# A new order for all engines from a corrected tally, and later v in four transfers, in a windowed attention with a gated feed-forward layer

## The chip, the cores and the metric

The kernel runs on one core of a Trainium2 chip. The metric is the device time of one execution in microseconds. It was 347.35 us in the median of three runs (346.08 to 350.0).

## The reference

Inputs are q, k and v of 8 batches, 8 heads, 576 positions and 64 dimensions in float32, a value weight and an output weight of 512 x 512, and a depthwise convolution of 5 taps on 512 channels.

```
scores = (q @ k.T) / 8, and only 0 <= i - j < 64 is kept
attn   = softmax(scores)                # the sum has 1e-9 added
x      = attn @ v                       # heads side by side: 8 x 576 x 512
gate   = sigmoid(sum over 5 taps of conv_w[tap] * x shifted)   # causal, per channel
out    = (gate * (x @ w_val)) @ w_out
```

The three weights come as float64 words and are taken apart in the kernel.

## The kernel before

**Attention.** The window is 64, so a block of 64 queries meets two blocks of keys. A score group (S, line 529) covers two query blocks of all 8 heads with 32 small float32 products of 64 x 32 by 96 columns. VectorE (DVE) adds the mask and takes the maximum (M, line 547), ScalarE (ACT) makes the exponent and the sums (X, line 559), GpSimd (POOL) and DVE make the reciprocal (Ra, Rb), one of DVE, POOL or ACT multiplies by it (N, lines 579 and 581), and DVE transposes (T, line 593). There are 36 score groups. A batch is cut into two halves of 256 and 320 positions (or 320 and 256), and for each half TensorE (PE) makes the product with v in many small matmuls (AV, line 630).

**Convolution.** Its taps run on DVE (C, line 718), but for three quarters of the first batch on PE, as products with diagonal matrices (K, line 693; the diagonals DG are built at line 897).

**Feed-forward.** x and h are each split into a high and a low part in float32r, and so are the two weights, so every product is three: V (line 772) and O (line 842) are runs of 12 matmuls. x is split by XH and XL, h by HH and HL (line 804).

**Weights.** A 512 x 512 weight comes as four column or row blocks. Each block passes through nine steps, named by a letter: `h` (head, lines 443 and 445), `k` (clamp, line 448), `b`, `c`, `H`, `p`, `l`, `r` (line 475) and `s` (line 478). w0 to w3 are the value weight, w4 to w7 the output weight, cw the convolution's.

**The order of the work.** It is written out by a planner in the program (`in_order`) before the kernel is built: each operation has a cost on each engine that may run it (`flex`, or one engine by `on`), a priority with a hand-searched adjustment for each operation (`adj`), its dependencies and its buffers. The planner goes through them with a clock of its own and gives each engine one list, which the chip then runs in order. Transfers are one more list, on the queue of SyncE (SP). The clock of the planner also holds `Fetch`: PE's instructions come in blocks of a given size (`block`), and a block that is run too soon after the last one is late. Where PE would be idle in the first 120 us, the planner puts in dummy products of the identity (`warm`, line 250), two rows in the profile for each. Loads are named LQ (q and k of one half), LV (v of a batch; of the first batch in two parts, LV0_0 and LV0_1) and LW (weights: the value weight in four quarters LW0_0 to LW1_1, the output weight in two halves LW2 and LW3), LC (the convolution's weights) and DO (output rows). A lower priority number goes first among those that are ready.

Of the kernel before, what the change touches and what calls it, by code (L numbers as in the profile page):

```python
# [29 lines left out]
    flex=dict(EO='AV', HH='AV', HI='AV', C='AV', EX='AV', XH='AVG', XL='GV', CC='AV', DG='GV', HL='GV', N='GVA', WR='GV', WH='AV', TL='AVG', WK='GV', HA='AV'),  # L30
# [17 lines left out]
    drain=165,  # L48
    held=30,
# [55 lines left out]
def in_order(ops, room):  # L105
# [8 lines left out]
    ready = {}  # L114
    for op in ops:
        if not op.left:
            for e in op.cost:
                ready.setdefault(e, []).append(op)
    out, done = [], set()
    bus = port_at = 0.0  # L120
    mode = "F"
    fetch = Fetch()
    since, until, margin, each = CFG["awake"]
    total = len(ops)

    shared = {}

    def earliest(op, e):
        t = max(free_at.get(e, 0.0), ready_time(op, e))
        if op.share is not None and e in op.on:  # L130

            t = max(t, shared.get((op.share, "V" if e == "A" else "A"), 0.0) + 60.0)
        if e in op.port:
            t = max(t, port_at)
        return t

    while len(out) < total:
        best = None
        for e, c in ready.items():
            c[:] = [op for op in c if op not in done]  # L140
            pick, cand = None, []
            for op in c:
                t = earliest(op, e)
                if len(op.cost) > 1 and e != min(
                        op.cost, key=lambda x: earliest(op, x) + op.cost[x] + CFG["bias"].get(x, 0)):
                    continue
                for kind, c_ in op.needs:
                    s = slots[kind]
                    t = max(t, s[c_ - 1]) if len(s) >= c_ else float("inf")
                if t == float("inf"):  # L150
                    continue
                late = 0.0
                if e == "P":
                    late = fetch.run(t, op.n, op.cost[e] / op.n, bus, False) - t - op.cost[e]
                k = (t + late - (CFG["wait"] if e == "P" and op.prio < CFG["ffn_prio"] else 0)
                     - (CFG["stay"] if e == "P" and "F" != mode and op.mode != "F" else 0), op.rank)
                cand.append((k, op))
# [10 lines left out]
        if e == "P" and op.mode != mode:  # L168
            t += CFG["drain"]
# [40 lines left out]
def tile_window_attention_gated_ffn(  # L210
# [134 lines left out]
    def at_of(g):  # L345
        return g * 12.0 / NB
# [653 lines left out]
```

## Time and profile before

| | |
|---|---|
| median of three runs | 347.35 us (346.08 to 350.0) |
| profiled execution | 345.73 us, span 343.9 us |
| mean granted TensorE clock | 0.979 |
| PE busy | 317.9 us (92%) |
| DVE busy | 269.4 us (78%) |
| ACT busy | 238.5 us (69%) |
| POOL busy | 175.7 us (51%) |

Busy is the time in which at least one instruction of that engine ran. Matmuls overlap, so the sum of their durations is more than the busy time. PEld is PE's weight loads, beside the matmuls. "issue" as the cause of a wait means that the engine waited for nothing that the profile shows. A releaser is inferred from semaphores. A granted clock of 1.00 is the upper of TensorE's two levels, 0.50 the lower.

### The profile page before, as it was taken

The page shows a single profiled execution, that of the slowest core. Times are in us where ns is not written, and L with a number is a line of the kernel's source. Part 1 is how long each engine was busy: PE and PEld are TensorE (multiplying, and loading weights), DVE is VectorE, ACT ScalarE, POOL GpSimd, SP SyncE. Part 2 cuts the span into 40 slices and gives each one's busy share as a digit, 9 for nine tenths or more (in the row PEclk, how much of TensorE's full clock was granted, in tenths as well). Part 3 has the DMA queues.
Part 4 walks back from the last instruction along what each step waited for, and adds up shares of the span by engine and source line. Part 5 has one row for each costly group of instructions (what it writes and reads, how often), then busy time and mean ns, then how long its engine had stood idle before and what let it go on. Part 6 is the DMA issues. An engine that isn't in the chain of part 4 may idle for free.

```text
span 343.9 us, 15255 instructions
## 1 busy us (share of the span) xinstructions
PE 317.9 (92%) x6280; PEld 277.2 (81%) x6280; DVE 269.4 (78%) x1088; ACT 238.5 (69%) x867; POOL 175.7 (51%) x225
## 2 busy tenths in 40 slices
PE   6687795989989999999999999989999999989995
PEld 5576584968978988898888888978898879978984
DVE  3887895779979796899798985979899878867300
ACT  1775795788588994487769796868639678734421
POOL 6355654554823663556523751857635264744510
PEclk9699997899999999999999999999999999999999
DMA  7969662273357031852564144750291100011012
GB/s 230 280 194 366 153 204 89 73 222 83 89 135 231 11 125 63 217 186 89 191 149 133 44 176 135 236 189 34 60 278 37 64 33 35 2 63 63 2 61 91
DMA packets 30117, 43.99 MB, mean 128 GB/s; under 512 B 2528, under 2 KB 23264, under 8 KB 30048
## 3 DMA queue, kind: packets, MB, share of 16 engines
q1 hardware_dynamic: 30048, 43.02, 41.1%
q8 instruction: 49, 0.80, 1.0%
q14 instruction: 20, 0.16, 0.1%
HBM read 33.57 MB, written 9.44 MB: 125 GB/s over the span
## 4 chain that ended last, share of the span: by engine, by line
PE 87%; DVE 4%; issue 3%; DMA 2%; POOL 1%; SPq 1%; ACT 0%; ACTq 0%
PE v L772 31%; PE o L842 30%; PE s L529 10%; PE av L630 10%; PE g L693 5%; DMA qk_b<-in_kT_dram 2%; DVE pb L547 2%; PE s L250 1%; POOL w3m L448 1%; PE g L692 0%; DVE pts L593 0%; PE g L250 0%; DVE wv_lo L478 0%; DVE xl L732 0%; SPq L373 0%
## 5 line engine op out<-in xcount | busy, mean ns | idle before, releaser
L559 ACT ACTIVATE pb<-pb,nm 128x96 f32<-128x96 f32 x288 | 103.8, 363 | 10.5 <-DVE nm L547 10.3
L718 DVE SCALAR_TENSOR_TENSOR gp<-av,cw,gp 128x256 f32<-128x256 f32 (+9 forms) x232 | 105.7, 507 | 3.7 <-ACT gp L260 3.1
L804 POOL TENSOR_TENSOR h_lo<-hf,h_hi 128x256 fp32r<-128x256 f32 (+2 forms) x79 | 54.3, 696 | 70.3 <-ACT h_hi L254 60.9
L772 PE MATMUL v<-xl,wv_hi 128*128 128x256 f32 (+1 forms) x256 | 78.5, 307 | 1.2 <-DVE hf L783 1.2
L772 PE MATMUL v<-xh,wv_hi 128*128 128x256 f32 (+1 forms) x256 | 76.0, 297 | 0.0
L772 PE MATMUL v<-xh,wv_lo 128*128 128x256 f32 (+1 forms) x256 | 75.8, 296 | 0.0
L547 DVE CUSTOM_DVE_ANT_0 pb<-s,mask 128x96 f32<-128x96 f32 x288 | 55.4, 252 | 9.9 <-PE s L529 9.8
L842 PE MATMUL o<-wo_hi,h_lo 128*128 128x512 f32 (+1 forms) x148 | 58.6, 396 | 0.0
L842 PE MATMUL o<-wo_lo,h_hi 128*128 128x512 f32 (+1 forms) x148 | 57.2, 387 | 0.0
L842 PE MATMUL o<-wo_hi,h_hi 128*128 128x512 f32 (+1 forms) x148 | 57.1, 386 | 0.0
L559 ACT ACTIVATION_READ_ACCUMULATOR pb<-pb,nm 128x1 f32 x288 | 54.1, 188 | 0.0
L772 PEld LDWEIGHTS v<-xl,wv_hi 128*128 128x128 f32 x256 | 49.1, 192 | 4.3 <-DVE hf L783 1.6
L581 POOL TENSOR_TENSOR pb<-pb,rc 128x384 f32<-128x384 f32 x48 | 40.4, 852 | 23.3 <-DVE rc L569 23.1
L772 PEld LDWEIGHTS v<-xh,wv_hi 128*128 128x128 f32 x256 | 49.1, 192 | 0.5
L772 PEld LDWEIGHTS v<-xh,wv_lo 128*128 128x128 f32 x256 | 49.1, 192 | 0.0
L254 ACT CAST h_hi<-hf 128x256 fp32r<-128x256 f32 (+2 forms) x73 | 27.0, 383 | 28.1 <-DVE hf L783 25.9
L593 DVE STREAM_TRANSPOSE pts<-pb 128x384 f32<-128x384 f32 (+1 forms) x80 | 39.5, 520 | 8.7 <-POOL pb L581 7.7
L529 PE MATMUL s<-k,q 64*32 64x96 f32 x2016 | 34.2, 251 | 7.3 <-issue 5.8
L630 PEld LDWEIGHTS av<-pts,v 32*64 32x64 f32 x2560 | 32.7, 130 | 9.9 <-issue 6.7
L630 PE MATMUL av<-pts,v 32*64 32x96 f32 (+2 forms) x2560 | 36.3, 246 | 4.5 <-issue 4.4
L529 PEld LDWEIGHTS s<-k,q 64*32 64x32 f32 x2016 | 25.9, 106 | 16.2 <-issue 14.2
L783 DVE SCALAR_TENSOR_TENSOR hf<-gp,v 128x320 f32<-128x320 f32 (+1 forms) x64 | 28.4, 446 | 12.2 <-PE v L772 9.0
(140 smaller groups left out, 454.5 us busy)
## 6 DMA issues: line engine op xcount, KB each, us to landing
out_dram<-ot SPq DMA_DIRECT2D x35, 256.0 KB, 2.5
v<-in_vw_dram SPq DMA_DIRECT2D x56, 144.0 KB, 3.5
k<-in_kT_dram SPq DMA_DIRECT2D x8, 640.0 KB, 7.1
q<-in_qT_dram SPq DMA_DIRECT2D x7, 640.0 KB, 4.7
q<-in_qT_dram SPq DMA_DIRECT2D x7, 512.0 KB, 3.8
k<-in_kT_dram SPq DMA_DIRECT2D x3, 768.0 KB, 7.2
st<-in_w_val_dram SPq DMA_DIRECT2D x4, 512.0 KB, 6.4
st<-in_w_out_dram SPq DMA_DIRECT2D x2, 1024.0 KB, 10.3
```

The source lines that it names most:

```text
L254: nc.scalar.copy(out=out, in_=in_)
L529: nc.tensor.matmul(sp_t[m, hh][c * Q:c * Q + Q, t, 0:KW], lhsT=q_t[u][r, c, q0:q0 + Q], rhs=k_t[u][r, c, q0:q0 + KW], start=True, stop=Tru ...
L547: nc.vector.tensor_tensor_reduce(out=pe[:, t, :], in0=sp_t[u][:, t, 0:KW], in1=mk[par if at[tt][1] == 0 else None], scale=-SCALE, scalar=3 ...
L559: nc.scalar.activation(out=pe[:, t, :], in_=pe[:, t, :], func=AF.Exp, scale=-1.0, bias=nm[:, t:t + 1], accum_out=su[:, t:t + 1])
L581: MUL[e](out=pe, in0=pe, in1=rc.unsqueeze(2).broadcast_to([P, GB, KW]))
L593: nc.vector.transpose(out=pts_t[un][:, hh, r0 * KW:(r0 + 2 * (t1 - t0)) * KW], in_=pe[:, 2 * t0:2 * t1, :].rearrange("p t n -> p (t n)"))
L630: nc.tensor.matmul(ap[hh * D:(hh + 1) * D, col:col + (rb - ra) * Q], lhsT=v_t[b][c * Q:c * Q + Q, kb % 2, hh, kb // 2, :], rhs=x[:, x0:x0 ...
L718: nc.vector.scalar_tensor_tensor(out=acc, in0=x, scalar=col, in1=acc, op0=ALU.mult, op1=ALU.add)
L772: nc.tensor.matmul(vp_t[u][:, 0:hs.stop - hs.start], lhsT=w[:, c, js], rhs=x[:, c, hs], start=(a + z == 0), stop=(a + z == NM - 1))
L783: nc.vector.scalar_tensor_tensor(out=hf[:, 0:n], in0=gp_t[b][:, jb, hs], scalar=1.0, in1=vp_t.pop(u)[:, 0:n], op0=ALU.add, op1=ALU.mult)
L804: SUB[e](out=h_of("lo")[:, jb, dst:dst + hi - lo], in0=hf_t[u][:, lo:hi], in1=h_of("hi")[:, jb, dst:dst + hi - lo].bitcast(F32))
L842: nc.tensor.matmul(op_t[key][:, 0:cs.stop - cs.start], lhsT=h[:, jb, col:col + P], rhs=w[:, jb, cs], start=(a + z == 0), stop=(a + z == NM ...
```

## The change

It changes the numbers from which the planner makes the order, and one kind of transfer.

- PE's counts: a dummy counts 4 instructions where it counted 2; a score group counts one more; a block is 255 instead of 256, and takes 3.1 us, or 3.5 beside transfers (3.3 and 5.0 before).
- V and O are two modes of PE, and a change between them costs 90 ns in the planner's clock; a bonus for staying in mode is given among S and AV alone.
- Transfers: each one counts by itself, at most eight are under way in the planner's clock, issue and bus times are new, and those that start between 1.5 and 12 us land 1.8 us later.
- The clamp `k` may run on DVE alone; the planner's cost of it on POOL is 1930 ns for a block instead of 700. The diagonals' costs are higher.
- The v of the batches 1 to 7 comes in four transfers of 288 KB instead of eight of 144 KB.
- Priorities of later q, k and v grow with 20 times the batch's place, so that any output row that is ready goes ahead of them.
- All adjustments in `adj` are new (1241 instead of 1400), and `on` fixes the engine of 40 operations instead of 153. With all this the order of every engine is new.

```diff
-    flex=dict(... TL='AVG', WK='GV', HA='AV'),
+    flex=dict(... TL='AVG', WK='V', HA='AV'),
+    turn=90,
-    adj={'LQ0_0_0': -36.5678, 'LQ0_0_1': -13.4464, 'LV0_0': -18.6685, 'LQ0_1_0': -20.7663, 'LV0_1': 79.0183, 'LQ1_0_0': -83.1783, ...
-         'LW0_0': -43.8261, 'LW0_1': -37.963, 'LW1_0': -11.9204, 'LW1_1': -12.5567, ...},
+    adj={'LQ0_0_0': -28.2358, 'LQ0_0_1': 4.60036, 'LV0_0': -1.90564, 'LQ0_1_0': 0.83759, 'LV0_1': 2.10201, ...},
-    block=(256, 192, 3300.0, 5000.0),
+    block=(255, 192, 3100.0, 3500.0),
+    ring=8,
...
-                     - (CFG["stay"] if e == "P" and "F" != mode and op.mode != "F" else 0), op.rank)
+                     - (CFG["stay"] if e == "P" and mode in "QC" and op.mode in "QC" else 0), op.rank)
...
-            t += CFG["drain"]
+            t += CFG["drain"] if "Q" in (op.mode, mode) or "C" in (op.mode, mode) else CFG["turn"]
...
-                t = max(t, fetch.run(lo, 2 * op.spare, each / 2, bus))
+                t = max(t, fetch.run(lo, 4 * op.spare, each / 4, bus))
...
-            end0 = t + issue
-            bus = max(bus, end0) + busy
-            free_at[e] = end0
-            end = bus + 1900.0
+            for _ in range(op.n):
+                t0 = max(free_at[e] if _ else t, ring.pop(0))
+                free_at[e] = t0 + issue / op.n
+                bus = max(bus, free_at[e]) + busy / op.n
+                end = bus + 1900.0 + (1800.0 if 1500.0 < t < 12000.0 else 0.0)
+                ring.append(end)
...
-                   prio=... at_of(b * NB + j0) - 16))
+                   prio=... LATE * at_of(b * NB + j0) - 16))
...
+                src = vw[b, c, W:2 * W].rearrange("(y p) (h x) -> p y h x", y=2, h=2)
+                dst = v_t[b][c * Q:c * Q + Q].rearrange("p y h n d -> p y h (n d)")
+                if hi - lo < NB:
+                    for y in range(2):
+                        nc.sync.dma_start(out=dst[:, y, :, lo * D:hi * D], in_=src[:, y, :, lo * D:hi * D])
+                else:
+                    nc.sync.dma_start(out=dst.rearrange("p y h x -> p y (h x)"), in_=src.rearrange("p y h x -> p y (h x)"))
...
-        k = op(name + "k", pick("WK", V=70 + 270 * c, G=150 + 550 * c), clamp, [a], prio=prio, port="VG")
+        k = op(name + "k", pick("WK", V=70 + 270 * c, G=150 + 1780 * c), clamp, [a], prio=prio, port="VG")
...
-            n=32 * 2 * GB // 2)
+            n=32 * 2 * GB // 2 + 1)
```

The bases of the first loads' priorities are unchanged: -112, -111 and -103 for the three parts of the first q and k; -131, -108, -107 and -106 for the four quarters of the value weight; -99 and -98 for the halves of the output weight; -100 and -85 for the two parts of the first v. The new adjustments of the four quarters are 18.2981, -2.10023, 0.69241 and -0.55226.

## Rows read from the trace of the kernel before

**Rows 1.** The page's parts 1 and 3: busy us of each engine; the instruction queue.

```profile
PE 317.9 (92%) x6280; PEld 277.2 (81%) x6280; DVE 269.4 (78%) x1088; ACT 238.5 (69%) x867; POOL 175.7 (51%) x225
...
q8 instruction: 49, 0.80, 1.0%
```

**Rows 2.** Windows by engine (length, busy, instructions); the third row the dummies alone.

```profile
0.00:84.00 84.00, 66.44 (x1506) 56.66 (x1507) 62.76 (x280) 59.30 (x245) 45.57 (x61) 0.92 0.63 188
84.00:340.00 256.00, 251.16 (x4776) 220.54 (x4774) 206.66 (x811) 178.61 (x622) 130.16 (x165) 1.00 0.36 109
...
0.00:344.00 344.00, 18.40 (x120) 17.02 (x120) 0.98 0.42 128
```

**Rows 3.** Waits of PE (total us, times, longest): whole span, then from 83 us.

```profile
PE s L529 <- issue: 5.8, 3, 3.0
PE av L630 <- issue: 4.4, 5, 1.3
...
PE av L630 <- issue: 3.3, 4, 1.3
PE s L529 <- issue: 1.3, 1, 1.3
```

**Rows 4.** PE's timeline at the longest and the last stop (start, us; idle before).

```profile
56.11 1.20 PE L529 MATMUL s<-k,q 64*32 64x96 f32 x44 [2.97 <-issue]
...
309.66 0.45 PE L630 MATMUL av<-pts,v 32*64 32x64 f32 x28 [1.34 <-issue]
```

**Rows 5.** Windows from stop to stop, and the block before the longest stop.

```profile
37.73:56.11 18.38, 15.41 (x381) 12.60 (x381) 14.41 (x88) 14.85 (x66) 11.32 (x11) 1.00 0.55 164
...
99.58:184.92 85.34, 84.56 (x1781) 73.93 (x1781) 75.25 (x317) 65.57 (x243) 41.92 (x56) 1.00 0.50 145
...
227.65:275.65 48.00, 47.64 (x1020) 41.56 (x1020) 43.33 (x174) 34.45 (x130) 24.31 (x33) 1.00 0.36 112
...
49.80:56.10 6.30, 3.34 (x130) 2.87 (x129) 3.46 (x20) 4.02 (x16) 5.16 (x5) 1.00 0.62 221
```

**Rows 6.** The chain that ended last, 25 to 28 us (start, us, what).

```profile
25.15 1.92 POOL w3m L448
27.07 0.80 POOL pb L581
```

**Rows 7.** The window of the lower clock (the column after POOL is the clock).

```profile
56.30:63.00 6.70, 5.47 (x65) 5.13 (x55) 4.87 (x25) 5.35 (x25) 1.29 (x3) 0.50 0.02 4
```

**Rows 8.** The chain: 24 V matmuls of the same half at either clock.

```profile
48.57 2.83 PE v L772 x24
...
58.54 5.09 PE v L772 x24
```

**Rows 9.** Timelines of POOL and DVE: the first and last clamp on POOL, one on DVE.

```profile
4.82 1.92 POOL L448 TENSOR_SCALAR w0m<-w0m 128x512 f32<-128x512 f32 x1 [0.37 <-DVE w0m L445]
...
77.95 2.03 POOL L448 TENSOR_SCALAR w7m<-w7m 128x512 f32<-128x512 f32 x1 [2.37 <-DVE w7m L445]
...
20.83 0.38 DVE L448 TENSOR_SCALAR w2m<-w2m 128x512 f32<-128x512 f32 x1
```

**Rows 10.** PE's timeline, the first three score groups; the first 10 us (last column GB/s).

```profile
8.82 0.99 PE L529 MATMUL s<-qk_b,qk_a 64*32 64x96 f32 x64 [2.11 <-DVE w0m L461]
...
12.12 1.53 PE L529 MATMUL s<-qk_b,qk_a 64*32 64x96 f32 x64 [0.87 <-DMA qk_b<-in_kT_dram]
...
17.93 1.31 PE L529 MATMUL s<-qk_a,qk_b 64*32 64x96 f32 x64
...
0.00:10.00 10.00, 6.28 (x94) 5.90 (x94) 3.70 (x9) 1.28 (x1) 5.84 (x21) 1.00 0.81 247
```

**Rows 11.** SP's longest wait in total; two O runs on the chain.

```profile
SPq L856 <- ACT ot L260: 90.8, 18, 16.9
...
93.16 2.76 PE o L842 x12
...
173.05 2.96 PE o L842 x12
```

More of the change, by code (lines that the diff above doesn't have):

```diff
@@ L29 @@
     gate_prio=-9,
-    flex=dict(EO='AV', HH='AV', HI='AV', C='AV', EX='AV', XH='AVG', XL='GV', CC='AV', DG='GV', HL='GV', N='GVA', WR='GV', WH='AV', TL='AVG', WK='GV', HA='AV'),
+    flex=dict(EO='AV', HH='AV', HI='AV', C='AV', EX='AV', XH='AVG', XL='GV', CC='AV', DG='GV', HL='GV', N='GVA', WR='GV', WH='AV', TL='AVG', WK='V', HA='AV'),
     gb=4,
@@ L51 @@
-    on={'cwk': 'G', 'cwH': 'A', 'cwr': 'G', 'cws': 'V', 'DG0': 'G', 'DG1': 'V', 'DG2': 'V', 'w0h': 'V', 'w0k': 'G', 'w0H': 'V', 'w0r': 'G', 'w0s': 'V', 'w1h': 'A', 'w1k': 'G', 'w1H': 'A', 'w1r': 'G', 'w1s': 'V', 'w2h': 'A', 'w2k': 'V', 'w2H': 'V', 'w2r': 'V', 'w3h': 'A', 'w3k': 'G', 'w3H': 'A', 'w3r': 'G', 'w4h': 'V', 'w4H': 'V', 'w5r': 'V', 'w6h': 'A', 'w6r': 'V', 'w7h': 'V', 'w7k': 'G', 'N(0, 0)': 'V', 'N(0, 1)': 'A', 'N(1, 0)': 'G', 'N(1, 1)': 'G', 'EX0_0': 'A', 'TL0_0': 'V', 'XH0_0': 'G', 'CC0_0_0': 'A', 'CC0_0_1': 'A', 'CC0_0_2': 'A', 'C0_0_3_4': 'A', 'XL0_0': 'V', 'N(2, 0)': 'G', 'N(2, 1)': 'A', 'N(3, 0)': 'G', 'N(3, 1)': 'A', 'N(4, 1)': 'A', 'EX0_1': 'A', 'HH0_0_0_0': 'A', 'HH0_0_1_0': 'A', 'HH0_0_2_0': 'V', 'HH0_0_3_0': 'V', 'N(5, 0)': 'A', 'N(5, 1)': 'G', 'N(6, 0)': 'G', 'N(7, 0)': 'A', 'N(7, 1)': 'A', 'HA1_1': 'A', 'C1_1_2_4': 'V', 'XL1_1': 'V', 'HH1_0_0_0': 'A', 'HH1_0_0_1': 'A', 'HH1_0_1_0': 'A', 'HL1_0_1_1': 'G', 'HL1_0_2_0': 'G', 'HL1_0_2_1': 'G', 'HH1_0_3_0': 'A', 'HH1_0_3_1': 'A', 'HH1_1_2_0': 'A', 'HL1_1_2_0': 'G', 'HH1_1_3_0': 'A', 'EO640_0': 'A', 'EO896_0': 'V', 'EO1024_0': 'V', 'C2_0_0_4': 'A', 'C2_0_1_4': 'A', 'C2_0_2_4': 'A', 'C2_0_3_4': 'A', 'XL2_0': 'G', 'EX2_1': 'A', 'HA2_1': 'V', 'XH2_1': 'G', 'C2_1_0_4': 'A', 'C2_1_2_4': 'A', 'C2_1_3_4': 'V', 'HH2_0_1_0': 'A', 'HL2_0_1_0': 'V', 'HL2_0_3_0': 'G', 'HH2_1_0_0': 'A', 'HH2_1_3_0': 'A', 'EO1152_0': 'A', 'EO1408_0': 'A', 'EO1536_0': 'A', 'N(15, 1)': 'G', 'EX3_0': 'V', 'TL3_0': 'V', 'C3_0_0_4': 'A', 'C3_0_2_4': 'A', 'C3_0_3_4': 'V', 'XL3_0': 'G', 'N(16, 0)': 'V', 'N(16, 1)': 'G', 'N(17, 0)': 'G', 'EX3_1': 'A', 'C3_1_0_4': 'V', 'XL3_1': 'V', 'HH3_0_1_0': 'V', 'HH3_0_1_1': 'A', 'HH3_1_1_0': 'A', 'EO1664_0': 'V', 'EO1792_0': 'A', 'EO2048_0': 'A', 'C4_0_0_4': 'A', 'C4_0_1_4': 'V', 'C4_0_3_4': 'A', 'N(20, 0)': 'A', 'HA4_1': 'A', 'XH4_1': 'A', 'C4_1_0_4': 'V', 'C4_1_2_4': 'V', 'C4_1_3_4': 'A', 'HH4_0_1_0': 'A', 'HH4_0_2_0': 'A', 'HH4_1_0_0': 'A', 'HH4_1_1_0': 'A', 'HH4_1_2_0': 'A', 'HL4_1_2_0': 'G', 'HH4_1_3_0': 'A', 'HL4_1_3_0': 'G', 'EO2304_0': 'A', 'EO2560_0': 'V', 'EX5_0': 'A', 'C5_0_0_4': 'A', 'C5_0_1_4': 'V', 'C5_0_2_4': 'A', 'C5_0_3_4': 'A', 'XL5_0': 'G', 'EX5_1': 'A', 'HA5_1': 'V', 'C5_1_0_4': 'A', 'C5_1_1_4': 'A', 'C5_1_2_4': 'V', 'C5_1_3_4': 'A', 'XL5_1': 'V', 'HH5_0_0_0': 'V', 'HH5_0_3_0': 'A', 'N(27, 0)': 'V', 'N(28, 1)': 'G', 'N(30, 1)': 'V', 'EX6_1': 'A', 'HA7_1': 'V'},
@@ new lines @@
+    on={'cwr': 'V', 'cws': 'V', 'DG0': 'V', 'DG2': 'V', 'w0r': 'G', 'w1H': 'V', 'w1r': 'V', 'w2h': 'A', 'w2H': 'V', 'w2r': 'V', 'w2s': 'V', 'w3h': 'V', 'w3r': 'V', 'w3s': 'V', 'w5H': 'A', 'N(0, 0)': 'G', 'N(0, 1)': 'A', 'XL0_0': 'V', 'N(2, 0)': 'G', 'N(2, 1)': 'G', 'N(4, 0)': 'V', 'XL0_1': 'V', 'HH0_0_0_0': 'A', 'HL0_0_1_0': 'G', 'EX2_1': 'A', 'HA2_1': 'A', 'C2_1_2_4': 'V', 'XL2_1': 'G', 'XL3_0': 'V', 'EX4_0': 'A', 'HA4_1': 'V', 'C4_1_1_4': 'A', 'EX5_1': 'A', 'C5_1_2_4': 'A', 'HH5_0_0_0': 'V', 'HH5_0_0_1': 'A', 'HH5_0_2_1': 'A', 'EX7_0': 'V', 'TL7_0': 'V', 'XL7_1': 'V'},
@@ L126, in in_order @@
     shared = {}
+    ring = [0.0] * CFG["ring"]
     def earliest(op, e):
@@ L326, in tile_window_attention_gated_ffn @@
     ops = []
+    LATE = 20
     def op(name, cost, emit, deps=(), take=(), free=(), prio=0, port="G", mode="F", n=0, share=None, on="AV"):
@@ L376, in load_qk @@
             j0 = c0 // W
-            o = op(f"LQ{b}_{z}_{n}", ("D", (2100 * NHP * (c1 - c0 + (W / 2 if n == 0 else 0)) / S, 1000)), emit,
-                   take=[("qk%d" % z, b)] if n == 0 and b else (),
-                   prio=CFG["lq0"][n + 2 * z] if b == 0 else CFG["lq"].get((b, z), at_of(b * NB + j0) - 16))
+            kb = NHP * P * 4e-3 * (2 * (c1 - c0) + (W if z and n == 0 else 0))
+            o = op(f"LQ{b}_{z}_{n}", ("D", (kb / (0.29 if c1 - c0 <= P else 0.34), 1060)), emit,
+                   take=[("qk%d" % z, b)] if n == 0 and b else (), n=2,
+                   prio=CFG["lq0"][n + 2 * z] if b == 0 else CFG["lq"].get((b, z), LATE * at_of(b * NB + j0) - 16))
             for j in range(j0, c1 // W):
@@ L390, in emit @@
             for c in range(NHP):
-                for y in range(2):
-                    nc.sync.dma_start(
-                        out=v_t[b][c * Q:c * Q + Q, y, :, lo:hi, :],
-                        in_=vw[b, c, W + y * Q:W + y * Q + Q].rearrange("p (h n d) -> p h n d", h=2, d=D)[:, :, lo:hi, :])
-        return op(f"LV{b}_{z}", ("D", (3900 * (hi - lo) / NB, 560 * 2 * NHP)), emit, take=[("v", b)] if z == 0 else (),
-                  prio=CFG["lv"].get((b, z), at_of(b * NB + lo) - 12))
+                src = vw[b, c, W:2 * W].rearrange("(y p) (h x) -> p y h x", y=2, h=2)
[5 more added lines that the diff above has]
+                    nc.sync.dma_start(out=dst.rearrange("p y h x -> p y (h x)"), in_=src.rearrange("p y h x -> p y (h x)"))
+        parts = 2 * NHP if hi - lo < NB else NHP
+        return op(f"LV{b}_{z}", ("D", (1024.0 * P * (hi - lo) / 320.0, 580 * parts)), emit, take=[("v", b)] if z == 0 else (), n=parts,
+                  prio=CFG["lv"].get((b, z), LATE * at_of(b * NB + lo) - 12))
     st_t = {}
@@ L422, in load_words @@
         if n >= 2:
-            return [op(f"LW{n}", ("D", (2930, 500)), lambda _: emit((0, 1)), take=big if n < 3 else (),
+            return [op(f"LW{n}", ("D", (2950, 560)), lambda _: emit((0, 1)), take=big if n < 3 else (), n=1,
                        prio=CFG["lw"][n + 2])] * 2
-        return [op(f"LW{n}_{z}", ("D", (1465, 500)), lambda _, z=z: emit((z,)), take=() if z else big,
+        return [op(f"LW{n}_{z}", ("D", (1480, 560)), lambda _, z=z: emit((z,)), take=() if z else big, n=1,
                    prio=CFG["lw"][2 * n + z]) for z in range(2)]
@@ L777, in ffn @@
                            take=[("ps_f", u)] if a == 0 else [],
-                           free=[], prio=prio, n=2 * len(part))
+                           free=[], prio=prio, mode="V", n=2 * len(part))
                 def e_hf(_, u=u, jb=jb, hs=hs):
@@ L845, in ffn @@
                            [o] + (need + sum(w_ops[1], []) if a == 0 else []),
-                           take=[("ps_f", key)] if a == 0 else [], prio=prio, n=2 * len(part))
+                           take=[("ps_f", key)] if a == 0 else [], prio=prio, mode="O", n=2 * len(part))
                 last_o.append(o)
@@ L856, in e_do @@
                     nc.sync.dma_start(out=out_f[key[0]:key[0] + P, cs], in_=ot_t.pop(key)[:, 0:cs.stop - cs.start])
-                op("DO%d_%d" % key, ("D", (750 / halves, 500)), e_do, [eo], free=[("w", key)], prio=aux)
+                op("DO%d_%d" % key, ("D", (750 / halves, 400)), e_do, [eo], n=1, free=[("w", key)], prio=aux)
         h_last[b] = last_o
@@ L876, in tile_window_attention_gated_ffn @@
     lws = sum((load_words(n) for n in range(4)), [])
-    lc = op("LC", ("D", (200, 500)), e_lc, prio=-99)
+    lc = op("LC", ("D", (200, 560)), e_lc, n=1, prio=-99)
     ch = const.tile([P, NCW], F32R, name="ch")
@@ L899, in e_dg @@
                    in1=cw[:, hp * TAPS:(hp + 1) * TAPS].unsqueeze(2).broadcast_to([P, TAPS, P]))
-        dgo[hp] = op(f"DG{hp}", pick("DG", V=740, G=1450), e_dg, [cwo, dgo.get(min(dgi)) if n else None],
+        dgo[hp] = op(f"DG{hp}", pick("DG", V=950, G=1700), e_dg, [cwo, dgo.get(min(dgi)) if n else None],
                      take=[] if n else [("v", "dg")], prio=CFG["dg"][n], port="VG")
```

2 lines of the change are left out of this document (1 added, 1 removed).

## The prediction

> **What bounds the kernel now.** I read the page's busy shares first [rows 1]. PE is busy for 317.9 us of the 343.9 us span, its weight loads overlap that, and no other engine passes 78%. Two windows [rows 2] part the span: in 0 to 84 us PE is busy for 66.4 us, from 84 to 340 us for 251.2 of 256.0 us. Part of the first is dummy products of the identity, 120 matmuls and 18.4 us over the whole span, which compute nothing [rows 2]. In the second part only PE's own work and PE's own stops set the time.
>
> The waits [rows 3] then say what stops PE. After 83 us no engine and no transfer does: the only entries are "issue", 3.3 us before AV products and 1.3 us before score products, in five stops. Over the whole span "issue" before these two kinds is 5.8 + 4.4 = 10.2 us in eight stops; the longest and the last stand in [rows 4].
>
> Where do they fall? Windows cut at the stops [rows 5] count matmuls and weight loads from one stop to the next: 381 + 381 = 762, 1781 + 1781 = 3562, 1020 + 1020 = 2040. These are 3, 14 and 8 times 254 to 255. So instructions arrive in blocks of about 256, and a stop is the wait for the next block when the last was run too fast. 49 packets of 0.80 MB on the instruction queue [rows 1] are 16 KB each, one for each block. Short instructions outrun it: in [rows 4] 44 score matmuls, which with their loads are 88 instructions, take 1.2 us, while a dozen O matmuls take 2.76 [rows 11].
>
> The Trainium skill speaks against that: "Runtime: NRT & Kernel Launch", section "Instruction fetch mechanics", has the sequencer fetch the next block of 256 while it runs the current one, and calls the fetch hidden, since issue is slower. The size agrees with these rows, the hiding does not. By that rule the 10.2 us would be no fetch, the corrected count would be worth nothing, and my sum would end near 344 instead of 337 us.
>
> Before 84 us the chain runs through DVE, POOL and ACT in turn, with PE on dummies; a piece of it is in [rows 6].
>
> **The change part by part.** The sum is made against the profiled execution, 345.73 us (span 343.9 and 1.8 around it). That is 1.6 us under the median of the runs shown, 347.35; I add it back at the end.
>
> *Instruction counts.* The tally decides where a score or AV run stands against the block borders, and it had the borders in the wrong places. A dummy counted 2, while its two matmuls and two loads are 4: 60 dummies make 120 uncounted. 36 score groups had one too few, 36. A block was 256 where 254 to 255 of the counted ones fit: 49 in 49 blocks. Together some 205, most of one block. So the old plan's care for the fetch was blind after its start, and its eight stops are what chance gave. With borders known, V or O products can be put where one comes. Bounds: all gone, -10.2; none gone, 0. Some will stay: the block of the 2.97 us stop lasted 6.3 us, from 49.8 to 56.1 us, with transfers at 221 GB/s beside it [rows 5], and the new tally takes 3.5 us for such a block (5.0 before). I take three stops left at the mean of 1.27: -10.2 + 3.8 = -6.4 us.
>
> *The half clock behind the longest stop.* From 56.3 to 63.0 us the granted clock is 0.50, the lower of the two levels; before it PE stood for 2.97 us [rows 4, 7]. In there 24 V matmuls take 5.09 us; the same 24 at 48.57 us took 2.83 [rows 8]: 2.26 us. If the stop goes, so should this. Bounds -2.3 and 0; I take -1.5, since thin stretches remain before 60 us.
>
> *Clamp from POOL to DVE.* Seven weight blocks are clamped on POOL, the first in 1.92 us and the last in 2.03; the one on DVE took 0.38 [rows 9]. Moved, they add 7 x 0.38 = 2.7 us to DVE, which is busy for 62.8 of the first 84 us [rows 2], and take 13.7 from POOL. At 25.15 us the clamp stands on the chain ahead of a normalization [rows 6]: 1.92 less 0.38 is -1.5. Two other blocks before 36 us and the small conv one add about 0.9 to DVE where no idle time takes them. Net -0.5; bounds -1.9 and +2.7.
>
> *Load order at the start.* From bases and adjustments in the diff the queue becomes: first q and k; weight quarters 1, 2, 4; second q and k; quarter 3; the q and k of the second half; v. Now quarter 1 is ahead of all, and two quarters, not four, are ahead of the second half. The first scores stand at 8.82 us; with 512 KB less ahead, at the 247 GB/s of the first 10 us [rows 10], they come up to 2.1 us sooner. The second scores, which wait for a transfer at 12.12 us, come 2.1 later, the third 1.0 MB or 4.2 us later [rows 10], but weights come earlier. DVE has work of both kinds, so one should pay for the other. Taken 0; bounds -3 and +4.2.
>
> *Later v, q and k.* Seven batches lose four issues each on SP, and the four left carry twice the bytes. SP waits 90.8 us for ACT's outputs alone [rows 11], so its issue time is covered: 0. The factor 20 puts a later load behind every output store that is ready first; a load queued behind a store that still waits would come late, by as much as SP's longest such wait, 16.9 us [rows 11]. Since now no PE wait after 83 us names a transfer, the loads have a lead; taken 0, bounds 0 and +7, half of that wait less a little.
>
> *Runs of V and O, engines left free.* An O of 12 matmuls takes 2.96 us behind scores and 2.76 elsewhere [rows 11], so ten such changes more or fewer are 2 us: taken 0, bounds -2 and +2. That 113 fewer operations are pinned to an engine moves work between DVE, ACT and POOL, which wait for PE after 84 us: 0, as long as DVE's 206.7 us of 256 [rows 2] doesn't grow by a quarter.
>
> **Sum.** 345.7 - 6.4 - 1.5 - 0.5 = 337.3 us for a profiled execution; with 1.6 for the median 338.9. I forecast 338.5.
>
> **Rivals.** *The stops move and none goes.* There are as many scores and AV products as before, and two groups side by side fill a block in 2 to 3 us. Eight stops at other borders, or by the page's rule stops that were no fetch at all, leave 345.7 less the clamp and perhaps the clock: 345 to 347 at the median. For it: the block time in the new tally is well under the 6.3 us seen. Against: the counted borders, which it now has nearly right. Chance 0.20.
>
> *The start slips (slower).* Place: the third scores, and the next batch's q and k. The third scores wait for 1.0 MB more, 4.2 us; the next batch's q and k now also stand behind the second part of the first v, 8 x 80 KB or 2.6 us at the same rate. If both lie on PE's way, 6.8 us are lost before the first V products, and since the second part is rigid, all of it reaches the end: 347.35 + 6.8 = 354 us with no stop gone, 348 with them at my value. It decides from the point where the third scores start after 22 us, not 17.93, and V's first products after 52, not 48.57. Against: DVE had enough to do then. Chance 0.15.
>
> *More than the sum.* The old tally knew neither the slow clamp nor the late first transfers. In the first 84 us PE is idle for 17.6 and on dummies for up to 18.4 [rows 2]; an order that fits both could bring the full second part forward by some 8 us, under a quarter of that: 338.5 - 8 = 330.5. Chance 0.12.
>
> **How the numbers follow.** The forecast keeps 0.53; by its own bounds it lies at 333 to 344. About 1% is what a measurement of this kernel can tell from no change, so faster is under 343.9 us and slower over 350.8. Faster: 0.50 of the forecast, the whole last rival, 0.02 of the first: 0.64. Slower: the slip without gain, 0.12, and 0.04 for a load held behind a store: 0.16. The rest, 0.20, is no change. The range goes from below the last rival's value to between no change and the slip: 328 to 350.
>
> **What would show it.** Right: three stops or fewer on "issue" before scores and AV, 4 us or less; no clock of 0.50 after 20 us; PE waiting for nothing else after 84 us; no clamp on POOL. Wrong: as many stops at other multiples of 256; a wait of PE for a transfer or for DVE between 12 and 60 us; V's first products after 50 us; a q or k load queued behind a waiting store.

## The result

The changed kernel takes 336.68 us in the median of four runs (334.88 to 337.48); the kernel before, 346.99 us. The ratio is 0.973 (95% interval 0.968 to 0.978). The profiled execution is 336.24 us, 9.5 less than that of before. The forecast was 338.5 us, between 328 and 350. In all that follows a median is over all runs of a kernel, while a ratio and its interval compare only runs within 1.5% of their kernel's fastest.

The page after, busy shares, answers to [rows 1]:

```profile
PE 320.7 (96%) x6326; PEld 280.8 (84%) x6326; DVE 272.4 (81%) x1098; ACT 237.3 (71%) x877; POOL 150.6 (45%) x214
```

PE is busy 320.7 us where it was 317.9, in a span 9.4 us shorter; of the 320.7, dummies take 6.1 us more than before. Windows of the changed kernel up to the end of its last matmul (length, busy of PE, PEld, DVE, ACT, POOL, then clock, DMA share, GB/s) answer to [rows 2, 7]; the third row is its dummies alone:

```profile
0.00:84.00 84.00, 74.59 (x1585) 65.32 (x1585) 71.50 (x301) 60.70 (x244) 31.64 (x54) 0.98 0.68 199
84.00:330.80 246.80, 246.07 (x4744) 215.52 (x4742) 200.91 (x798) 176.21 (x634) 118.92 (x161) 1.00 0.36 109
...
0.00:335.00 335.00, 24.48 (x166) 23.48 (x166) 0.99 0.44 131
...
56.30:63.00 6.70, 4.95 (x170) 3.99 (x170) 5.46 (x16) 5.60 (x22) 3.33 (x5) 1.00 0.62 152
```

From 84 us on, PE is idle for 0.7 us where it was idle for 4.8 of 256.0 [rows 2]. The clock is 1.00 in the window where it was 0.50. Dummies take 24.5 instead of 18.4 us, so of PE's greater share in the first window part is dummies. The waits of PE from 33 us to the last matmul (total, times, longest) answer to [rows 3]:

```profile
PE s L541 <- issue: 1.7, 1, 1.7
PE av L642 <- issue: 0.7, 1, 0.7
PE av L642 <- DVE gp L730: 0.2, 1, 0.2
PE s L541 <- DVE nm L559: 0.2, 1, 0.2
```

Eight stops on "issue" with 10.2 us have become two with 2.4. By the prediction's count, scores and AV over the whole span, they have become three with 4.2, since an AV product waits 1.77 us at 29.57 us. The kernel before has such a stop there too, 1.76 us at 30.80 us, but ahead of a dummy, which that count leaves out. With it, 12.0 us have become 4.2. The timeline of PE and the windows around the stops answer to [rows 4, 5]:

```profile
22.69 3.62 PE L256 MATMUL av<-ident 128*128 128x128 f32 x30
...
29.57 0.42 PE L642 MATMUL av<-pts,v 32*64 32x64 f32 x21 [1.77 <-issue]
29.92 7.92 PE L256 MATMUL g<-ident 128*128 128x128 f32 x54
...
56.39 1.33 PE L642 MATMUL av<-pts,v 32*64 32x96 f32 x94 [0.68 <-issue]
57.66 0.68 PE L541 MATMUL s<-k,q 64*32 64x96 f32 x34
59.99 0.56 PE L541 MATMUL s<-k,q 64*32 64x96 f32 x30 [1.66 <-issue]
```

```profile
29.57:56.39 26.82, 26.14 (x507) 23.66 (x507) 23.07 (x108) 19.83 (x75) 9.65 (x12) 0.94 0.49 146
56.39:59.99 3.60, 1.94 (x128) 1.68 (x127) 2.57 (x6) 2.79 (x10) 2.27 (x3) 1.00 0.35 95
...
31.40:34.30 2.90, 2.90 (x15) 2.90 (x15) 2.70 (x7) 2.52 (x4) 0.00 (x0) 0.50 0.43 94
```

The stops that are left stand at block borders too: ahead of the one at 56.39, 507 + 507 = 1014 = 4 x 253.5 instructions (matmuls and weight loads) lie in the first window, and 128 + 127 = 255 lie between it and the last stop; that block took 3.6 us. The last row shows that the lower clock is not gone altogether: behind the stop at 29.57 us it is 0.50 from 31.4 to 34.3 us, while PE runs dummies.

Counted from PE's first instruction, stops stand at the same place in both orders. Up to the stop at 56.11 us before, and up to the one at 56.39 us after, PE has done 982 matmuls and 983 loads:

```profile
0.00:56.10 56.10, 40.87 (x982) 35.45 (x983) 41.48 (x209) 37.06 (x163) 32.27 (x48) 0.94 0.76 232
```

```profile
0.00:56.38 56.38, 48.79 (x982) 44.55 (x983) 45.49 (x210) 37.30 (x153) 20.39 (x40) 0.97 0.67 205
```

### The profile page after: what moved, and what is told of

It reads as the page before. It is cut to its first block, busy times and chain, and to the rows that moved or that the text cites. A ratio compares the mean times of both kernels' runs of the same rounds, so it can differ in the third digit from the quotient of the medians.

```text
span 334.5 us, 15330 instructions
## 1 busy us (share of the span) xinstructions
PE 320.7 (96%) x6326; PEld 280.8 (84%) x6326; DVE 272.4 (81%) x1098; ACT 237.3 (71%) x877; POOL 150.6 (45%) x214
## 4 chain that ended last, share of the span: by engine, by line
PE 90%; DVE 6%; issue 2%; ACT 1%; POOL 0%; ACTq 0%; POOLq 0%; DVEq 0%
PE o L854 29%; PE v L784 29%; PE s L541 10%; PE av L642 10%; PE g L705 5%; PE s L256 3%; PE g L256 2%; DVE gp L730 2%; DVE pb L559 2%; PE av L256 1%; DVE hf L795 1%; PE g L704 0%; DVE pts L605 0%; ACT pts L260 0%; DVE gp L267 0%
## 5 line engine op out<-in xcount | busy, mean ns | idle before, releaser
L784 PE MATMUL v<-xl,wv_hi 128*128 128x256 f32 (+1 forms) x256 | 77.2, 302 | 0.0
L784 PE MATMUL v<-xh,wv_hi 128*128 128x256 f32 (+1 forms) x256 | 75.2, 294 | 0.1
L854 PE MATMUL o<-wo_hi,h_lo 128*128 128x512 f32 (+1 forms) x148 | 59.5, 402 | 0.3
L784 PEld LDWEIGHTS v<-xl,wv_hi 128*128 128x128 f32 x256 | 48.2, 188 | 2.7
L784 PEld LDWEIGHTS v<-xh,wv_lo 128*128 128x128 f32 x256 | 48.1, 188 | 0.6 <-issue 0.6
L784 PEld LDWEIGHTS v<-xh,wv_hi 128*128 128x128 f32 x256 | 48.1, 188 | 0.2
L260 ACT CAST h_hi<-hf 128x256 fp32r<-128x256 f32 (+2 forms) x71 | 25.0, 377 | 23.1 <-DVE hf L795 23.1
L266 ACT ACTIVATE ot<-o 128x512 f32<-128x512 f32 (+1 forms) x34 | 19.7, 578 | 25.5 <-PE o L854 23.0
L541 PE MATMUL s<-k,q 64*32 64x96 f32 x2016 | 32.6, 248 | 1.8 <-issue 1.7
L854 PEld LDWEIGHTS o<-wo_hi,h_lo 128*128 128x128 f32 x148 | 27.8, 188 | 7.6 <-issue 0.6
## 6 DMA issues: line engine op xcount, KB each, us to landing
out_dram<-ot SPq DMA_DIRECT2D x35, 256.0 KB, 2.1
```

Source lines behind the costliest of these rows:

```text
L260: nc.scalar.copy(out=out, in_=in_)
L541: nc.tensor.matmul(sp_t[m, hh][c * Q:c * Q + Q, t, 0:KW], lhsT=q_t[u][r, c, q0:q0 + Q], rhs=k_t[u][r, c, q0:q0 + KW], start=True, stop=Tru ...
L784: nc.tensor.matmul(vp_t[u][:, 0:hs.stop - hs.start], lhsT=w[:, c, js], rhs=x[:, c, hs], start=(a + z == 0), stop=(a + z == NM - 1))
L854: nc.tensor.matmul(op_t[key][:, 0:cs.stop - cs.start], lhsT=h[:, jb, col:col + P], rhs=w[:, jb, cs], start=(a + z == 0), stop=(a + z == NM ...
```

## Experiments

All of them keep the computation. Except in the two on the tally, the planner's order is frozen: only what its list emits is edited, and in experiment 5 the place of the first loads.

**1. Move the borders, touch nothing else.** If the stops are block borders in bad places, a few instructions more at the start of PE's list must move all of them. The lengths of all blocks in the two traces, with every border moved by the same number, say how much would stop at each number. For 76 instructions more they say: the old order gains, the new order loses. The edit in the kernel before (S0 is the first score group; in the changed kernel the second, S1):

```diff
+        for n in range(more[0]):
+            r, c = 0, n % 4 * 32
+            nc.tensor.matmul(t[c:c + 32, n // 4 % 4, 0:96], lhsT=ident[r:r + 64, 0:32], rhs=ident[r:r + 64, 0:96],
+                             start=True, stop=True, tile_position=(r, c))
+        more[0] = 0
...
-        warm[0] = o.spare
+        warm[0], more[0] = o.spare, 19 * (o.name == 'S0')
```

A first pair had another edit: it put in small dummies of 128 x 128 by one column and left out some of the others, 76 instructions more in all. For the kernel before:

> The kernel before, its order untouched, but PE runs 76 instructions more ahead of the first scores: 4 of the 15 dummies there are left out and 23 small ones of one column put in, in time in which PE waits for data anyway. Every block border moves 76 instructions forward in the order. Theory (borders): from the block lengths in the trace of before, with a block that runs in under 3.1 us (4.5 beside busy transfers) taken as a stop, the stops after 33 us fall from 10.8 us by this count (10.2 seen) to 1.6, with one left near 97 us; with the half clock and the wait for DVE behind the 2.97 us stop gone too, 347 becomes 335 to 338. Rival (the gain of the change is in its order, its loads and its clamp; the stops are no fetch): 346 to 348.

It took 340.2 us, ratio 0.984 (0.979 to 0.989): faster, but less than said. PE's timeline shows a flaw of the experiment: the small dummies took 0.21 us a row, and the first scores began at 16.02 us, not 8.82 [rows 10].

```profile
6.28 9.81 PE L254 MATMUL s<-ident 128*128 128x1 f32 x46
16.02 1.53 PE L533 MATMUL s<-qk_b,qk_a 64*32 64x96 f32 x64
```

For the changed kernel:

> The changed kernel, its order untouched, with the same 76 instructions more ahead of the second scores (8 of 22 dummies left out, 27 small ones put in). Theory (borders): its order is made for its own borders; by the same count the stops rise from 2.0 us to 15.5, so 336.7 becomes 347 to 351, about what before had or more, with some eleven stops of 1 to 1.6 us. Rival (order, loads or clamp make the gain): 336 to 338.

Its median was 360.0 us (353.6 to 361.2), with the same flaw in it; there is no ratio for it. The second pair uses the 19 products of the diff above, which have the scores' shape.

> The same question as the first pair, without its flaw: there the small dummies of one column took 0.21 us a row and put the first scores 7 us later. Now the kernel before gets 19 products of 64 x 32 by 96 columns (76 instructions, about 1 us) in the 2.1 us in which PE waits for the first scores' data; no dummy is left out, its order is untouched. Theory (borders): first scores at 8.8 us as before, one or two stops after 33 us (1.6 us by the block count, near 97 us), no half clock at 56 us: 332 to 337, so the old order with other borders is as fast as the new order. Rival (the new order, its loads and clamp have a good part of the gain): 340 to 343. Rival (the start only): 346.

It took 333.9 us (332.99 to 335.44), ratio 0.964 (0.959 to 0.968). Its waits of PE from 33 us to the end, and its window where the clock had been 0.50:

```profile
PE v L778 <- DVE hf L789: 2.2, 2, 1.2
PE s L535 <- DVE nm L553: 1.4, 2, 1.0
PE s L535 <- issue: 1.1, 2, 0.9
PE av L636 <- issue: 1.0, 1, 1.0
```

```profile
56.00:63.00 7.00, 7.00 (x190) 5.72 (x189) 6.89 (x13) 6.97 (x27) 5.10 (x5) 1.00 0.58 148
```

"issue" is 2.1 us, the half clock is gone. The wait for DVE at the first hf, which I had thought to go with the stop, is still there.

> The changed kernel, order untouched, with the same 19 products ahead of the second scores, 1 us or less of PE's time. Theory (borders): about ten stops of 1 to 1.7 us after 33 us, 12 to 15 us more, perhaps a half clock behind one: 347 to 352. Rival (order, loads or clamp): 336 to 338.

It took 353.5 us, ratio to before 1.012 (1.003 to 1.021), so by the ratios 13 us more than the changed kernel without the 19 products. From 33 us on, and with two of the windows from stop to stop:

```profile
PE s L547 <- issue: 7.1, 5, 1.8
PE av L648 <- issue: 5.4, 4, 2.0
PE v L790 <- issue: 1.4, 2, 0.9
```

```profile
99.05:132.66 33.61, 31.84 (x636) 27.86 (x637) 30.46 (x141) 24.98 (x102) 17.65 (x27) 1.00 0.45 129
...
208.72:229.07 20.35, 18.64 (x383) 16.09 (x384) 16.92 (x63) 12.49 (x43) 9.21 (x10) 1.00 0.54 157
```

13.9 us of stops, at 5 times 254.6 and 3 times 255.7 instructions. Besides, the third scores waited 2.1 us for a transfer in this execution, and after 33 us the clock was 0.50 twice for 3.4 us, behind the stops at 59.6 and 132.7 us.

> The kernel before with 48 such products (192 instructions, 2 to 3 us) at the same place. Theory (borders): the block count gives 20.2 us of stops instead of 10.8, in fourteen or so: 354 to 358, of which up to 1 us is the products' own time. Rival (more instructions at the start are good or bad by themselves, whatever their number): the same sign as with 76.

It took 364.1 us, ratio 1.040 (1.033 to 1.048), more than said; the profiled execution was 359.4. Its stops from 33 us on:

```profile
PE av L636 <- issue: 14.0, 9, 3.5
PE s L535 <- issue: 5.2, 3, 2.6
PE o L848 <- issue: 0.3, 1, 0.3
```

Side by side, with the stops after 33 us:

| kernel | block lengths say, us | "issue" seen, us | median, us | ratio to before |
|---|---|---|---|---|
| before | 10.8 | 10.2 | 347.0 | 1 |
| before, 76 more | 1.6 | 2.1 | 333.9 | 0.964 |
| before, 192 more | 20.2 | 19.5 | 364.1 | 1.040 |
| changed | 2.0 | 2.4 | 336.7 | 0.973 |
| changed, 76 more | 15.5 | 13.9 | 353.5 | 1.012 |

The sign depends on the number and on the order, and the size follows the count. This shows the cause: the same 19 products make one order 13 us faster and the other 13 us slower. With them the kernel before stops at 27.29 us behind 952 matmuls and loads and at 91.50 us behind 3495, where without them it stops at 30.80 us behind 952 and at 99.57 us behind 3495: the places in PE's count stay, and other work stands there. And the old order with moved borders is faster than the new one, so nothing else in the new order was needed for the gain.

**2. The counts alone, and all but the counts.** Here the planner makes new orders.

```diff
-    block=(256, 192, 3300.0, 5000.0),
+    block=(255, 192, 3300.0, 5000.0),
...
-                t = max(t, fetch.run(lo, 2 * op.spare, each / 2, bus))
+                t = max(t, fetch.run(lo, 4 * op.spare, each / 4, bus))
...
-            n=32 * 2 * GB // 2)
+            n=32 * 2 * GB // 2 + 1)
```

> The kernel before with the three counts alone corrected in its tally (a dummy 4, a score group one more, a block 255), everything else as before, the old adjustments among it; the planner makes a new order of it. Theory (borders): two stops or three after 33 us where eight were, if the planner's care for the fetch works with adjustments that were searched for other borders; 338 to 344, since the rest of the order now fits them less well. Rival (the counts are worth nothing without a new search): 345 to 352.

It took 362.4 us, ratio 1.046 (1.040 to 1.051). Its waits of PE from 33 us, the first five and all on "issue":

```profile
PE v L772 <- DVE hf L783: 4.1, 4, 2.1
PE av L630 <- DVE gp L718: 3.8, 2, 3.5
PE g L693 <- ACT pts L254: 2.6, 1, 2.6
PE o L842 <- DVE ot L261: 2.5, 2, 1.8
PE v L772 <- POOL xl L732: 2.0, 1, 2.0
PE s L529 <- issue: 1.1, 1, 1.1
...
PE v L772 <- issue: 0.4, 1, 0.4
...
PE av L630 <- issue: 0.2, 1, 0.2
```

The stops fell to 1.7 us, as the theory has it, but PE now waits 15 us and more for DVE, ACT and POOL, which it never did after 83 us before. My time was wrong by 18 us. I take it that adjustments searched for one order are worth little in another; which of them cost what was not traced.

> The changed kernel with the three old counts in its tally (a dummy 2, a score group one less, a block 256), all else new, the new adjustments among it; the planner makes a new order of it. Theory (borders, and adjustments that hold only for the order they were searched for): as with the counts alone, the adjustments no longer fit; stops of the fetch return, five or more after 33 us, and PE waits for other engines too: 345 to 365. Rival (the counts make no difference): 336 to 338.

This reverses the diff above in the changed kernel. It took 348.7 us, ratio to before 1.003 (0.998 to 1.008), but not in the way that I gave: one stop of 1.8 us, and waits for DVE and ACT.

```profile
PE av L642 <- DVE gp L730: 2.6, 2, 1.9
PE v L784 <- DVE hf L795: 2.3, 2, 2.0
PE av L642 <- issue: 1.8, 1, 1.8
```

So the old counts too gave an order with few stops, and this run doesn't show that the right counts are needed. It hardly could: it has 83 dummies (166 rows), and by the prediction's own tally 166 + 36 + 49 = 251 instructions go uncounted by the end, nearly a whole block, after which the borders fall where they would have. That is an argument and not a measurement. The time, 3% over the changed kernel's, again goes with adjustments that were searched for another order.

**3. The clamp.** One line chooses the engine that runs it; the place in the order stays.

```diff
-        o.emit(o.engine)
+        o.emit('V' if o.name[0] in 'cw' and o.name[-1] == 'k' else o.engine)
```

In the changed kernel 'G' stands for 'V'.

> The kernel before, its order untouched, but every clamp runs on DVE at the place where the order had it on POOL. Theory (as predicted): -0.5 us, between -1.9 and +2.7. Rival (the slow clamp was what held the start): 3 us or more faster, with the first V products 3 us earlier than 48.2 us.

Ratio 0.9955 (0.9912 to 0.9998): -1.6 us, with an interval from -3.1 to 0, inside the bounds. The medians of all runs, 346.15 and 346.42, differ by 0.3 only, so a gain by the clamp alone is not shown. The first run of V came at 49.84 us in its profile, not earlier than the 48.22 of before.

> The changed kernel, its order untouched, with every clamp on POOL instead of DVE. Theory (as predicted, the other way round): +0.5 us, between -2.7 and +1.9; 336 to 339. Rival (the clamp's move matters in the order made for it, since weights wait for it at the start): +3 us or more, 340 and up.

338.1 us, ratio to before 0.972 (0.966 to 0.979), where the changed kernel has 0.973: no difference that shows.

**4. v in four transfers.** The new `emit` of v in the old order.

> The kernel before, its order untouched, with v of batches 1 to 7 in four transfers instead of eight. Theory: 0, within 1 us of 347, since SP's issue time is covered and v is loaded a batch ahead. Rival (the transfers matter): 2 us or more, either way.

Ratio 1.005 (1.002 to 1.009), 0.7 to 3 us slower. No wait of PE in its profile names a transfer of v. Where those 2 us come from was not found; it is no part of the gain.

**5. The load order at the start.** The first 14 loads, in the changed kernel's order, go to the head of SP's list.

```diff
+    start = ['LQ0_0_0', 'LW0_0', 'LW0_1', 'LW1_1', 'LQ0_0_1', 'LW1_0', 'LQ0_1_0', 'LV0_0', 'LC',
+             'LW2', 'LW3', 'LV0_1', 'LQ1_0_0', 'LQ1_1_0']
+    order.sort(key=lambda o: start.index(o.name) if o.name in start else len(start))
```

> The kernel before with the first 14 loads in the changed kernel's order on SP's queue (q and k first, weight quarters 1, 2, 4 ahead of the second q and k, quarter 3 ahead of the second half's, the rest of the first v ahead of the next batch's q and k); every engine's own order untouched. Theory (the load order is about neutral): first scores near 5 us instead of 8.8, second and third 2 to 4 us later, the later scores of the next batch up to 4 us later; 345 to 350, 0 to +3. Rival (the new load order is part of the gain): 343 or less.

351.9 us, ratio 1.013 (1.008 to 1.018): 4.5 us slower, more than I had said. Two rows of PE's timeline show it:

```profile
13.86 0.76 PE L250 MATMUL s<-ident 128*128 128x128 f32 x2 [5.53 <-DVE nm L547]
...
40.30 0.74 PE L529 MATMUL s<-k,q 64*32 64x96 f32 x32 [4.26 <-DMA k<-in_kT_dram]
```

Ahead of the second scores PE waits 5.53 us for DVE (0.98 before), whose frozen list has the first weight quarter's steps in front, and that quarter now lands later. The next batch's scores wait 4.26 us for their k, behind the rest of the first v. That is a place that the slower rival named, and V's first products come at 55.54 us, 7.3 later than the 48.22 of before, where the rival had 6.8. The stops on "issue" after 33 us are 7.1 us here, 3.1 less than before, so the end comes less late. In the changed kernel the same scores start at 41.99 us without such a wait: its order has other work ahead of them.

**6. The two gains together.** The 19 products and the clamp on DVE, in the kernel before.

> The two edits of the kernel before that were faster, together: 19 products ahead of the first scores, and the clamp on DVE; order, loads and v as before. Theory: the stops are worth 12 us and the clamp 0 to 2, and they don't touch each other: 331 to 334, faster than both kernels. Rival (the clamp's small gain was chance): 333 to 335, the same as with the products alone.

332.2 us (331.3 to 332.79), ratio 0.956 (0.951 to 0.960), faster than both kernels. From the 333.9 of the products alone it is 1.7 us, but the intervals of the two ratios touch: that the clamp adds to the products is likely and not shown.

## Why the prediction was right

*Instruction counts.* What the step says of the cause held, and nearly its size: -6.4 forecast; by the prediction's own count 10.2 less 4.2, so -6.0, and with the stop ahead of a dummy 12.0 less 4.2, so -7.8. I expected three stops with 3.8 us, and three with 4.2 came. I had counted some 205 instructions missing from the old tally; by the block lengths the old order does best with about 76 more, that is 180 of a block back, which fits. That block borders cost these stops is shown by experiment 1. That it was the corrected count which led the planner around them is argued: the counts alone cut the stops to 1.7 us in a slower order, but the old counts with all the rest new had 1.8. The rule of the Trainium skill ("Runtime: NRT & Kernel Launch", section "Instruction fetch mechanics") that the fetch is hidden by the rate of issue does not hold here: 76 instructions that compute nothing moved the time by 13 us down in one order and by 13 us up in the other.

*The half clock.* -1.5 forecast; the one behind the longest stop went whole, which is -2.26 by [rows 8]. The moved borders alone removed it as well. In the changed kernel with 76 more one came back behind each of two stops. But "no clock of 0.50 after 20 us" did not come true: it is 0.50 from 31.4 to 34.3 us, behind the stop at 29.57 us.

*The clamp.* -0.5 forecast; 0 to -3 in the old order, nothing in the new one. The 13.7 us taken from POOL are no gain by themselves; [rows 1] has it busy for 51% only.

*The load order.* This term was mis-sized: 0 taken, bounds -3 and +4.2; measured by itself in the old order +4.5 (2.8 to 6.3). I took DVE's other work for a cover, but PE waited for DVE too, and for k where I had put only 2.6 of the 6.8 us, at the next batch's q and k. How much of this price the changed kernel pays is not shown: its first scores come at 4.71 us instead of 8.82, the second at 14.00 instead of 12.12, the next batch's nine later than the 33 us of before, and V's first products nevertheless 2 us earlier, at 46.25 us.

*Where the 9.5 us lie.* The window from 84 us to the last matmul is 256.3 us before and 246.8 after. 4.1 of it are idle time of PE, which stood in stops [rows 3]. The rest, 5.4, is work done before 84 us: V and O alone by then (before, V; after, V and O):

```profile
0.00:84.00 84.00, 9.18 (x54) 8.78 (x55) 0.92 0.63 188
```

```profile
0.00:84.00 84.00, 10.22 (x75) 9.63 (x75) 0.98 0.68 199
...
0.00:84.00 84.00, 3.31 (x12) 2.10 (x12) 0.98 0.68 199
```

21 V matmuls at 0.13 us and a dozen O at 2.76 make 5.5. Of these, stops give 5.5 - 2.3 = 3.2, the clock 2.3 [rows 8], and a wait for DVE that is gone 1.2:

```profile
PE v L772 <- DVE hf L783: 1.2, 1, 1.2
```

That is 6.7, so by difference 1.3 are lost elsewhere before 84 us. The trace has one place of that size: the 54 dummies behind the stop at 29.57 us, part of them at 0.50, take 7.92 us, and at the pace of the 30 in 3.62 us at 22.69 they would take 6.5. The chain that ended last runs through them up to 37.84 us, though the first diagonals for the convolution behind them are written by 34.70. That these 1.4 us are the ones missing is an estimate; no run separates them.

*Later v, q and k* cost 0 by my sum; alone, v's new form cost 2 us, and the reason is open. *The rivals:* "stops move" fell with the 4.2 us that are left of 10.2; "more than the sum" did not come, though the old order with moved borders shows that 334 was to be had; "the start slips" is real as a mechanism and too small to turn the sign.

*How near it came, and the signs.* Part of the nearness of 338.5 to 336.7 is luck: the load order was taken at 0 for a reason that experiment 5 does not bear out, and the 1.2 us of the wait for DVE were in no term. Of the signs, "4 us or less" was missed by 0.2 and the one on the clock by the stretch at 31.4 us. The sign of being wrong, a wait for DVE or a transfer between 12 and 60 us, came too (0.98 us for DVE ahead of 15.98 us), but the kernel before has the like (1.02 ahead of 14.68), so it could tell nothing.

What the forecast did not see is that the new order was not needed. About 1% lies between the changed kernel (0.973) and the old order with its borders moved (0.964), and this 1% is what the new order costs. By 84 us the old order with moved borders has done 84 V matmuls and a dozen O, the new one 75 and a dozen; nine V matmuls at 0.13 us are 1.2 of some 3 us. The rest was not traced.

## What to carry to other kernels

When PE stops for "issue", count its matmuls and weight loads between the stops. If the counts are multiples of one block, short instructions have outrun the fetch, and a handful of harmless instructions early in PE's list, their number chosen from the block lengths in the trace, can be worth more than a new order. A priority list that was searched on one tally should not be run on another, even a better one, without a new search: the counts alone cost 4.6%.

## What was not expected

- Products of one column by 128 rows were hardly cheaper than products of 128 columns. The kernel before with small dummies has both, one behind the other, at a clock of 1.00:

```profile
1.42 5.06 PE L251 MATMUL s<-ident 128*128 128x128 f32 x22 [1.42 <-POOL ident masks.py:199]
6.28 9.81 PE L254 MATMUL s<-ident 128*128 128x1 f32 x46
```

```profile
6.30:16.00 9.70, 9.70 (x47) 9.70 (x46) 2.58 (x5) 0.67 (x1) 3.78 (x4) 1.00 1.09 316
```

  That is 0.23 us a row with 128 columns and 0.21 with one. The weight loads, of 128 columns either way, are busy all through that window (the second pair of numbers).
- Of the stops measured, the longer ones stood beside busy transfers. With 192 more instructions PE stopped for 3.54 us in the first window, where DMA moved 224 GB/s; before, it stopped for 1.34 us in a block at 67 GB/s (the second window, [rows 4]):

```profile
150.40:155.90 5.50, 1.98 (x146) 1.85 (x146) 2.72 (x20) 4.67 (x19) 1.59 (x2) 0.99 0.62 224
```

```profile
306.60:309.60 3.00, 1.73 (x133) 1.57 (x133) 0.49 (x1) 0.79 (x2) 0.32 (x1) 1.00 0.18 67
```
